# A fifth buffer of probabilities, the exponential ahead of the copies in even slots, early sign bits read a slot behind their product, row sums in six columns

## The chip, the core and the metric

One core of a Trainium2 chip runs the whole program. The engines named here are PE (TensorE's matmuls), PEld (its weight loads), DVE (VectorE), ACT (ScalarE), POOL (GpSimd) and SP (the queue that issues most of the DMAs). The metric is the device time of one execution in microseconds; a kernel's time is the median of several executions.

## What is computed

Attention within hash buckets, for 4 batches and 8 heads of 768 positions with 64 channels, and then a gated block on the 512 channels of the heads side by side:

```python
q_bits = (np.einsum('bhsd,dk->bhsk', q, proj) > 0)          # 6 signs; k_bits likewise
mask = q_bucket[:, :, :, None] == k_bucket[:, :, None, :]
scores = np.where(mask, scale * np.matmul(q, k.transpose(0, 1, 3, 2)), -1e9)
scores = scores - np.max(scores, axis=-1, keepdims=True)
attn = np.exp(scores)
attn = attn / (np.sum(attn, axis=-1, keepdims=True) + 1e-09)
x = np.matmul(attn, v)                                      # then heads side by side: B, 768, 512
gate = sigmoid(sum(conv_w[k] * shifted(x, k) for k in range(5)))
out = (gate * (x @ w_val)) @ w_out
```

## The kernel before

The work is cut into 192 tiles: 32 units (a batch and a head), and six tiles of 128 query rows in each. A tile's scores are 128 by 768. One loop runs over k, and what an iteration issues I call a slot. The order in which instructions are written is the order in which PE, ACT, DVE and POOL run them; SP's DMAs are ordered by a scheduler. Every engine takes its instructions strictly in turn, and one that waits holds all behind it.

A slot works on several tiles at once. In slot k:

- ACT copies the transposed probabilities of tile k-4 out of PSUM (`keep_transposed`, L348, two copies into `pt`).
- DVE takes the row maxima of tile k (`nm`, L297). In even slots it adds 1e-9 to the row sums of the pair k-2, k-1 (`row_sums`, L321, out of `sm` into `s1`; a profile names it `s`) and takes their reciprocals (`ri`, L325). It makes the factor `gs` (L303) and the shift `nb` (L307) of tile k.
- POOL scales the probabilities of tile k-2 by the reciprocals (L330).
- PE computes the scores of tile k+1 (L291) into one of two buffers `s`; the exponential of tile k-1 must have read that one.
- ACT takes the exponential of tile k (L315), with the shift as its bias, into a buffer `p`, and sums its rows on the way into `sm`. There are four `p` (`bufs=LAG + 1`, LAG is 3).
- PE takes a piece of other work: a piece of the gated block of an earlier batch (four matmuls, L424 or L449), in some early slots a product for sign bits, and in odd slots two steps of attention times values (L362, into `av`). DVE, POOL and ACT take pieces of weight conversion, convolution (L393) and so on.
- PE transposes the probabilities of tile k-3 (L339), three into each of two PSUM buffers `tp`; each must have been emptied by a copy of tile k-4.

When the last step of attention times values of a unit has been issued (an odd slot, k = 1 mod 6), ACT copies `av` into `x` (L370, two copies), behind that slot's exponential. So in the next even slot, k = 2 mod 6, these two copies stand ahead of whatever ACT does first.

The gated block of a batch can start when its eight heads are done, so up to about 190 us PE has no pieces of it. In those first slots the eight weight parts are converted on DVE, ACT and POOL, through the one PSUM buffer `m`.

The signs of q and k against the projections are folded into the scores as 12 more rows. For units 0 to 15 they come from `bits` (L229 the product into `m`, L232 the compare on DVE). For units 16 to 31 a generator, `early_bits`, makes them ahead of time: it loads four units' halves (L246), multiplies them (L251, into `m`), compares on DVE (L254, out of `m` into `ht`) and stores the result in DRAM (L256). It takes one step in each slot k with 6 <= k < 60 and k mod 6 in (3, 4); a step that multiplies also compares and stores.

An output block is copied out of PSUM into one of two buffers `o` (L455 on DVE, L457 on ACT) and stored by L459.

Of the kernel before, what the change touches and what calls it, by code (L numbers as in the profile page):

```python
# [8 lines left out]
FP32 = mybir.dt.float32  # L9
# [17 lines left out]
def kernel(  # L27
# [26 lines left out]
    vp = ctx.enter_context(tc.tile_pool(name="vp", bufs=2))  # L54
    pp = ctx.enter_context(tc.tile_pool(name="pp", bufs=LAG + 1))
    small = ctx.enter_context(tc.tile_pool(name="small", bufs=6))
# [5 lines left out]
    wst = ctx.enter_context(tc.tile_pool(name="wst", bufs=2))  # L62
    op = ctx.enter_context(tc.tile_pool(name="op", bufs=2))

# [171 lines left out]
    def early_bits():  # L236

        for i in range(16, len(units), 4):
            u = dram.tile([P, S], FP32, name="ud")
            rows = []  # L240
            for hf, name in enumerate(("hh", "hl")):
                yield
                rows.append([hp.tile([P, HS], FP32R, name=name).bitcast(FP32) for _ in range(4)])
                for jj, t in enumerate(rows[-1]):
                    b, h = units[i + jj]
                    nc.sync.dma_start(out=t, in_=qk[b, h, :, hf * HS:(hf + 1) * HS])  # L246
            for hf in range(2):
                yield
                z = ps_m.tile([P, 512], FP32, name="m")
                for jj, t in enumerate(rows[hf]):  # L250
                    nc.tensor.matmul(out=z[32 * jj:32 * jj + 32, 0:HS], lhsT=proj_sb, rhs=t, start=True, stop=True,  # L251
                                     tile_position=(0, 32 * jj))
                t = hp.tile([P, HS], FP32, name="ht", bufs=2)
                nc.vector.tensor_scalar(out=t.bitcast(FP32R), in0=z[:, 0:HS], scalar1=rows_sb[:, 0:1],  # L254
                                        scalar2=rows_sb[:, 1:2], op0=ALU.is_ge, op1=ALU.mult)
                nc.sync.dma_start(out=u[:, hf * HS:(hf + 1) * HS], in_=t)  # L256
            early[i] = u

# [50 lines left out]
    def exponentials(k):  # L309
        s, nb = ss.pop(k), nbs.pop(k)  # L310
        p = pp.tile([P, 2, HS], FP32, name="p")
        if k % 2 == 0:
            cur["sm"] = small.tile([P, 2, 2], FP32, name="sm")
        sm = cur["sm"]
        nc.scalar.activation(out=p, in_=s[:, :, 0:HS], func=AF.Exp, bias=nb, scale=gs.pop(k), accum_out=sm[:, k % 2, 0:1])  # L315
        ps[k] = (p.rearrange("p a b -> p (a b)"), sm)


    def row_sums(k):
        sums[k] = small.tile([P, 2, 2], FP32, name="s1")  # L320
        nc.vector.tensor_scalar(out=sums[k][:, :, 0], in0=ps[k][1][:, :, 0], scalar1=1e-9, scalar2=None, op0=ALU.add)  # L321

    def recip(k):
        ri = small.tile([P, 2], FP32, name="ri")
        nc.vector.reciprocal(out=ri, in_=sums.pop(k)[:, :, 0])  # L325
        rcs[k], rcs[k + 1] = ri[:, 0:1], ri[:, 1:2]
# [82 lines left out]
    def moe(b, xs_, g):  # L409
# [30 lines left out]
        def outp(o, tb):  # L440
# [4 lines left out]
            for hi, wi in ((0, 0), (0, 1), (1, 0)):  # L445
# [6 lines left out]
                later()  # L452
            ob = op.tile([P, 512], FP32, name="o")
            if cur["gates"]:
# [46 lines left out]
    with tc.manual_schedule(engines=ENGINES):  # L501
# [10 lines left out]
        step(weights[1])  # L512
        ahead = [early_bits()]
        for k in range(N + LAG + 1):
            if 0 <= k - LAG - 1:
                keep_transposed(k - LAG - 1)
# [18 lines left out]
            if k < N:  # L535
                exponentials(k)
            if k >= 60 or k % 2:
                step(convs)
# [9 lines left out]
            step(preps)  # L548
            if 6 <= k < 60 and k % 6 in (3, 4):
                step(ahead)  # L550
# [72 lines left out]
```

## Time and profile before

| | us |
|---|---|
| median of 3 runs (620.15 to 621.71) | 621.56 |
| the profiled execution | 621.24 |
| its span, from the first to the last instruction | 619.2 |
| PE busy in the span | 585.0 |
| PE idle until scores could overwrite a buffer that an exponential read | 16.9 |
| DVE busy | 434.5 |
| ACT busy | 420.3 |
| POOL busy | 387.6 |

The TensorE clock granted was 0.997 of full speed. In a row of the timeline stand the start in us from the span's start, the time taken, the engine, the line, the operation, the output and inputs, the count of instructions merged, and in brackets the engine's idle time ahead of it with what ended it. In a row of the waits stand who waited for whom, then the us in total, the number of times, and the longest.

### The profile page before, as it was taken

What the parts mean: (1) busy time and instruction counts of PE and PEld (TensorE: products, weight loads), DVE (VectorE), ACT (ScalarE), POOL (GpSimd) and SP (SyncE); (2) the same over time, 40 slices, a digit from 0 to 9 for tenths busy, and PEclk for the clock granted to TensorE, in tenths of its full rate; (3) what the DMA queues carried; (4) which work ended last, traced back from release to release, by engine and by line L of the source; (5) the groups of instructions that cost most, each with busy time, mean ns of one, the idle gap of its engine ahead of it and who ended that gap; (6) DMA issues with size and microseconds to landing.
All of it is one profiled execution on the core that took longest, in us unless ns stands there. A gap on an engine that the chain in (4) does not pass through costs nothing.

```text
span 619.2 us, 10665 instructions
## 1 busy us (share of the span) xinstructions
PE 585.0 (94%) x3496; PEld 421.4 (68%) x3496; DVE 434.5 (70%) x1017; ACT 420.3 (68%) x881; POOL 387.6 (63%) x373
## 2 busy tenths in 40 slices
PE   5799998989899999999999999999999999999997
PEld 2665655556567776776668787777667777775895
DVE  5787889898885866668575867668665877665532
ACT  2786777677778676777787676777787766765400
POOL 3575777677866765578665777468764776544321
PEclk9899999999999999999999999999999999999999
DMA  7575767473533334243434234333422213200111
GB/s 228 167 209 168 216 170 208 129 202 82 132 82 74 79 77 130 73 108 83 125 80 115 55 83 123 87 112 83 108 70 78 68 43 92 66 19 1 51 52 51
DMA packets 29030, 64.64 MB, mean 104 GB/s; under 512 B 4936, under 2 KB 10056, under 8 KB 28976
## 3 DMA queue, kind: packets, MB, share of 16 engines
q1 hardware_dynamic: 28832, 63.93, 37.7%
q8 instruction: 28, 0.46, 0.3%
q14 instruction: 26, 0.21, 0.1%
q10 hardware_dynamic: 144, 0.03, 0.0%
HBM read 30.60 MB, written 7.86 MB: 62 GB/s over the span
## 4 chain that ended last, share of the span: by engine, by line
PE 71%; ACT 14%; DVE 11%; issue 2%; DMA 2%; SPq 0%; POOL 0%; ACTq 0%; DVEq 0%; POOLq 0%
PE av L362 19%; PE s L291 17%; PE tp L339 13%; PE m L449 8%; PE m L424 7%; ACT p L315 6%; ACT pt L348 4%; DVE nm L297 3%; ACT x L370 2%; DVE g L393 2%; PE tp L424 1%; PE tp L449 1%; PE s L449 1%; PE m L229 1%; PE s L424 1%
## 5 line engine op out<-in xcount | busy, mean ns | idle before, releaser
L330 POOL TENSOR_SCALAR p<-p,ri 128x768 f32<-128x768 f32 x192 | 205.0, 1072 | 157.7 <-DVE nb L307 131.3
L297 DVE TENSOR_REDUCE nm<-s 128x1 f32<-128x768 f32 x192 | 182.6, 951 | 63.9 <-PE s L291 63.5
L348 ACT COPY pt<-tp 128x384 f32<-128x384 f32 x384 | 165.7, 485 | 81.7 <-PE tp L339 80.9
L315 ACT ACTIVATE p<-s,nb,gs 128x768 f32<-128x768 f32 x192 | 192.7, 1003 | 40.5 <-DVE nb L307 35.6
L339 PEld LDWEIGHTS tp<-ident,p 128*128 128x128 f32 x1152 | 129.2, 141 | 71.8 <-issue 45.2
L339 PE MATMUL tp<-ident,p 128*128 128x128 f32 x1152 | 163.8, 278 | 2.8 <-ACT pt L348 2.2
L362 PE MATMUL av<-pt,vt 128*64 128x384 f32 x768 | 144.9, 498 | 0.0
L291 PE MATMUL s<-ak,aq 76*128 76x384 f32 x384 | 117.7, 387 | 19.6 <-ACT p L315 16.9
L291 PE MATMUL s<-bk,bq 128*128 128x384 f32 x384 | 100.6, 343 | 0.4 <-DVE bq L277 0.4
L362 PEld LDWEIGHTS av<-pt,vt 128*64 128x64 f32 x768 | 46.9, 136 | 63.0 <-issue 62.9
L291 PEld LDWEIGHTS s<-ak,aq 76*128 76x128 f32 x384 | 59.0, 193 | 35.6 <-ACT p L315 31.8
L393 DVE SCALAR_TENSOR_TENSOR g<-x,cw_sb,g 128x768 f32<-128x768 f32 x64 | 77.3, 1208 | 2.2 <-POOL g L391 2.1
L291 PEld LDWEIGHTS s<-bk,bq 128*128 128x128 f32 x384 | 71.2, 192 | 0.8 <-issue 0.8
L198 POOL TENSOR_TENSOR bq<-r,aq 128x768 fp32r<-128x768 f32 x31 | 57.5, 1853 | 0.1
L435 POOL TENSOR_TENSOR hl<-ht,hh 128x384 fp32r<-128x384 f32 x32 | 32.2, 1006 | 39.4 <-DVE hh L433 39.4
L370 ACT COPY x<-av 64x384 f32<-64x384 f32 x64 | 30.4, 474 | 30.9 <-PE av L362 30.2
L383 POOL TENSOR_TENSOR xl<-x,xh 128x384 fp32r<-128x384 f32 x32 | 33.4, 1059 | 18.0 <-DVE xh L382 18.0
L424 PE MATMUL m<-xh,wv 128*128 128x384 f32 x200 | 42.7, 337 | 0.0
L307 DVE TENSOR_SCALAR nb<-nm,gs 128x1 f32<-128x1 f32 x192 | 40.2, 209 | 3.5
L315 ACT ACTIVATION_READ_ACCUMULATOR p<-s,nb,gs 128x1 f32 x192 | 39.1, 203 | 0.0
L429 DVE TENSOR_TENSOR ht<-m,g 128x384 f32<-128x384 f32 x25 | 13.9, 556 | 35.7 <-PE m L424 29.3
L449 PE MATMUL m<-wo,hh 128*128 128x512 f32 x144 | 38.1, 394 | 0.0
(86 smaller groups left out, 483.7 us busy)
## 6 DMA issues: line engine op xcount, KB each, us to landing
r<-in_qk_dram SPq DMA_DIRECT2D x32, 384.0 KB
vt<-in_v_dram SPq DMA_DIRECT2D x16, 384.0 KB
out_dram<-o SPq DMA_DIRECT2D x24, 256.0 KB
ak<-aq SPq DMA_DIRECT2D x31, 192.0 KB
bk<-aq SPq DMA_DIRECT2D x31, 192.0 KB
bk<-bq SPq DMA_DIRECT2D x31, 192.0 KB
bq<-aq SPq DMA_DIRECT2D x31, 192.0 KB
hh<-in_qk_dram SPq DMA_DIRECT2D x16, 192.0 KB
```

What stands on the lines that cost most here:

```text
L198: nc.gpsimd.tensor_tensor(out=bq, in0=r, in1=aq.bitcast(FP32), op=ALU.subtract)
L291: nc.tensor.matmul(out=s[:, hf, 0:HS], lhsT=lq[0:n, qs], rhs=rk[0:n, hf * HS:(hf + 1) * HS], start=n == M, stop=n == P)
L297: nc.vector.tensor_reduce(out=nm, in_=s[:, :, 0:HS], axis=AX.XY, op=ALU.max, negate=True)
L315: nc.scalar.activation(out=p, in_=s[:, :, 0:HS], func=AF.Exp, bias=nb, scale=gs.pop(k), accum_out=sm[:, k % 2, 0:1])
L330: nc.gpsimd.tensor_scalar(out=p, in0=p, scalar1=rcs.pop(k), scalar2=1.0, op0=ALU.mult, op1=ALU.mult)
L339: nc.tensor.transpose(out=tp[:, n * P:(n + 1) * P], in_=p[:, kb * P:(kb + 1) * P], identity=ident)
L348: nc.scalar.copy(out=pt[:, :, qo:qo + P], in_=tp[:, 0:HS].rearrange("p (a b) -> p a b", b=P))
L362: nc.tensor.matmul(out=av[s * D:(s + 1) * D, 0:HS], lhsT=vt[:, kb, hh * D:(hh + 1) * D], rhs=pt[kb // 3][:, kb % 3, :], start=(kb == 0), s ...
L370: nc.scalar.copy(out=x[hh * D:(hh + 1) * D, o:o + HS], in_=av[s * D:(s + 1) * D, 0:HS])
L393: nc.vector.scalar_tensor_tensor(out=g, in0=x[:, k:k + S], scalar=w, in1=g, op0=ALU.mult, op1=ALU.add)
L424: nc.tensor.matmul(out=acc[:, 0:HS], lhsT=wv[wi][:, c, j * P:(j + 1) * P], rhs=xs_[(c, o)][xi], start=(m == 0), stop=(m == 11))
L449: nc.tensor.matmul(out=acc, lhsT=hs[(o, j)][hi][:, tb * P:(tb + 1) * P], rhs=wo[wi][:, j, :], start=(m == 0), stop=(m == 11))
```

## The change

Five things change.

1. There are five buffers `p` instead of four, and one `o` instead of two. At the end of the program (`cur["end"]`) output blocks go through the `p` buffers.
2. In even slots `keep_transposed(k-4)` is issued behind the exponential of tile k. In odd slots it stays ahead.
3. `early_bits` has a step for the product and a step of its own for the compare and the store. The loads of a group are issued all eight at once, in the step of the last compare of the group before. The steps are taken in slots of a list `look`.
4. The row sums are written in six columns: the pair of sums three times over.
5. The reciprocal reads the first two of the six.

```diff
-    pp = ctx.enter_context(tc.tile_pool(name="pp", bufs=LAG + 1))
+    pp = ctx.enter_context(tc.tile_pool(name="pp", bufs=LAG + 2))
...
-    op = ctx.enter_context(tc.tile_pool(name="op", bufs=2))
+    op = ctx.enter_context(tc.tile_pool(name="op", bufs=1))
...
+        rows = rows_of(16)
+        for i in range(16, len(units), 4):
+            u = dram.tile([P, S], FP32, name="ud")
             for hf in range(2):
                 yield
+                z = product(rows[hf])
+                yield
                 t = hp.tile([P, HS], FP32, name="ht", bufs=2)
                 nc.vector.tensor_scalar(out=t.bitcast(FP32R), in0=z[:, 0:HS], scalar1=rows_sb[:, 0:1],
                                         scalar2=rows_sb[:, 1:2], op0=ALU.is_ge, op1=ALU.mult)
                 nc.sync.dma_start(out=u[:, hf * HS:(hf + 1) * HS], in_=t)
+            if i + 4 < len(units):
+                rows = rows_of(i + 4)
             early[i] = u
...
-        sums[k] = small.tile([P, 2, 2], FP32, name="s1")
-        nc.vector.tensor_scalar(out=sums[k][:, :, 0], in0=ps[k][1][:, :, 0], scalar1=1e-9, scalar2=None, op0=ALU.add)
+        sums[k] = small.tile([P, 6], FP32, name="s1")
+        nc.vector.tensor_scalar(out=sums[k], in0=ps[k][1][:, :, 0].unsqueeze(1).to_broadcast([P, 3, 2]), scalar1=1e-9,
+                                scalar2=None, op0=ALU.add)
...
-            ob = op.tile([P, 512], FP32, name="o")
+            if cur["end"]:
+                ob = pp.tile([P, 2, HS], FP32, name="p").rearrange("p a b -> p (a b)")[:, 0:512]
+            else:
+                ob = op.tile([P, 512], FP32, name="o")
...
+        look = [10] + [k for k in range(12, 50) if k % 6 in (3, 4) and k // 6 not in (3, 7)] + list(range(51, 59))
         for k in range(N + LAG + 1):
-            if 0 <= k - LAG - 1:
+            if 0 <= k - LAG - 1 and (k % 2 or k >= N):
                 keep_transposed(k - LAG - 1)
...
             if k < N:
                 exponentials(k)
+                if k % 2 == 0 and 0 <= k - LAG - 1:
+                    keep_transposed(k - LAG - 1)
...
-            if 6 <= k < 60 and k % 6 in (3, 4):
+            if k in look:
                 step(ahead)
```

Here `rows_of(i)` issues the eight loads of a group and `product(rows)` the four matmuls of a half into `m`.

ACT's order around the end of a unit's attention (slots k = 1, 2, 3 mod 6), before:

```order
L315 ACTIVATE p_835,sm_798<-s_792,nb_828,gs_825 128x768
L370 COPY x_605<-av_687 64x384 x2
L348 COPY pt_819<-tp_843 128x3x128
L348 COPY pt_820<-tp_847 128x3x128
L315 ACTIVATE p_869,sm_870<-s_830,nb_862,gs_857 128x768
L348 COPY pt_819<-tp_877 128x3x128
L348 COPY pt_820<-tp_881 128x3x128
L315 ACTIVATE p_899,sm_870<-s_864,nb_892,gs_889 128x768
```

And of the change:

```order
L325 ACTIVATE p_835,sm_796<-s_790,nb_828,gs_825 128x768
L381 COPY x_613<-av_692 64x384 x2
L325 ACTIVATE p_867,sm_868<-s_830,nb_860,gs_855 128x768
L359 COPY pt_819<-tp_843 128x3x128
L359 COPY pt_820<-tp_847 128x3x128
L359 COPY pt_819<-tp_877 128x3x128
L359 COPY pt_820<-tp_881 128x3x128
L325 ACTIVATE p_899,sm_868<-s_862,nb_892,gs_889 128x768
```

The exponential of the even slot now comes directly behind the two copies into `x`, and the four copies of two tiles' transposes follow each other.

PE's order at k = 15 and 16, with the first early product (`hh`), before:

```order
L229 MATMUL m<-r,proj_sb 32x384 x4
L362 MATMUL av<-pt,vt 64x384 x4
L339 MATMUL tp<-ident,p 128x128 x6
L291 MATMUL s<-ak,aq 128x384 x2
L291 MATMUL s<-bk,bq 128x384 x2
L251 MATMUL m<-hh,proj_sb 32x384 x4
L339 MATMUL tp<-ident,p 128x128 x6
```

And of the change:

```order
L229 MATMUL m<-r,proj_sb 32x384 x4
L250 MATMUL m<-hh,proj_sb 32x384 x4
L373 MATMUL av<-pt,vt 64x384 x4
L350 MATMUL tp<-ident,p 128x128 x6
L301 MATMUL s<-ak,aq 128x384 x2
L301 MATMUL s<-bk,bq 128x384 x2
L350 MATMUL tp<-ident,p 128x128 x6
```

The early product has moved from the even slot 16 into the odd slot 15, directly behind the other sign product into `m`.

DVE's order at k = 21 and 22, where a compare stood, before:

```order
L382 CAST xh<-x 128x384 x2
L254 TENSOR_SCALAR ht<-m,packed 128x384
L297 TENSOR_REDUCE nm<-s 128x1
L321 TENSOR_SCALAR s_937<-sm 128x2
L303 TENSOR_SCALAR gs<-nm 128x1
```

And of the change:

```order
L393 CAST xh<-x 128x384 x2
L307 TENSOR_REDUCE nm<-s 128x1
L331 TENSOR_SCALAR s_924<-sm 128x6
L313 TENSOR_SCALAR gs<-nm 128x1
L336 RECIPROCAL ri<-s_924 128x2
```

The compare has left this place, so nothing stands between the casts and the maxima of tile 22, and the row sums have their six columns.

More of the change, by code (lines that the diff above doesn't have):

```diff
@@ L236, in early_bits, with rows_of @@
     def early_bits():
-        for i in range(16, len(units), 4):
-            u = dram.tile([P, S], FP32, name="ud")
+        def rows_of(i):
             rows = []
             for hf, name in enumerate(("hh", "hl")):
-                yield
                 rows.append([hp.tile([P, HS], FP32R, name=name).bitcast(FP32) for _ in range(4)])
@@ L246, in early_bits, with product @@
                     nc.sync.dma_start(out=t, in_=qk[b, h, :, hf * HS:(hf + 1) * HS])
+            return rows
+        def product(rows):
+            z = ps_m.tile([P, 512], FP32, name="m")
+            for jj, t in enumerate(rows):
+                nc.tensor.matmul(out=z[32 * jj:32 * jj + 32, 0:HS], lhsT=proj_sb, rhs=t, start=True, stop=True,
+                                 tile_position=(0, 32 * jj))
+            return z
+        rows = rows_of(16)
+        for i in range(16, len(units), 4):
+            u = dram.tile([P, S], FP32, name="ud")
             for hf in range(2):
                 yield
[L249 to L252, printed above, removed]
+                z = product(rows[hf])
+                yield
                 t = hp.tile([P, HS], FP32, name="ht", bufs=2)
@@ L319, in row_sums @@
     def row_sums(k):
-        sums[k] = small.tile([P, 2, 2], FP32, name="s1")
-        nc.vector.tensor_scalar(out=sums[k][:, :, 0], in0=ps[k][1][:, :, 0], scalar1=1e-9, scalar2=None, op0=ALU.add)
+        sums[k] = small.tile([P, 6], FP32, name="s1")
+        nc.vector.tensor_scalar(out=sums[k], in0=ps[k][1][:, :, 0].unsqueeze(1).to_broadcast([P, 3, 2]), scalar1=1e-9,
+                                scalar2=None, op0=ALU.add)
     def recip(k):
         ri = small.tile([P, 2], FP32, name="ri")
-        nc.vector.reciprocal(out=ri, in_=sums.pop(k)[:, :, 0])
+        nc.vector.reciprocal(out=ri, in_=sums.pop(k)[:, 0:2])
         rcs[k], rcs[k + 1] = ri[:, 0:1], ri[:, 1:2]
```

## Prediction

> **What bounds the kernel now.** I read the busy time by stage first, then the waits, then single slots in the timeline. A slot is one tile k of the 192; "even" and "odd" are k's. The stages (columns: stretch in us, its length, then busy time of PE, PEld, DVE, ACT and POOL, clock, DMA share, GB/s):
>
> ```profile
> 20.00:190.00 170.00, 155.01 (x978) 99.90 (x978) 143.41 (x336) 129.54 (x278) 119.60 (x116) 0.99 0.56 156
> 190.00:560.00 370.00, 364.90 (x2203) 272.70 (x2200) 254.05 (x613) 272.01 (x572) 243.87 (x230) 1.00 0.33 84
> ```
>
> So TensorE sets the pace. Up to 190 us, before the second part's matmuls join, it idles 15.0 of 170 us and VectorE is close behind (84% busy). From 190 to 560 us it idles 5.1 of 370, and there only its own queue counts: whatever makes it wait once is not made up. The waits:
>
> ```profile
> ACT p L315 <- DVE nb L307: 35.6, 45, 6.0
> PE s L291 <- ACT p L315: 16.9, 34, 2.0
> DVE ht L254 <- PE m L251: 6.2, 6, 1.6
> PE tp L339 <- ACT pt L348: 2.2, 7, 0.8
> ```
>
> What the change goes after is in the second row: scores that wait for an exponential. What it may disturb is in the last: transposes wait almost never for ScalarE's copies.
>
> An ordinary even slot of the first stage (k=24), by engine:
>
> ```profile
> 73.00 0.87 PE L339 MATMUL tp<-ident,p 128*128 128x128 f32 x6
> 73.63 0.59 PE L291 MATMUL s<-ak,aq 76*128 76x384 f32 x2
> 74.41 0.82 PE L339 MATMUL tp<-ident,p 128*128 128x128 f32 x6
> 75.48 0.62 PE L291 MATMUL s<-ak,aq 76*128 76x384 f32 x2 [0.25 <-ACT p L315]
> ...
> 73.58 0.86 ACT L348 COPY pt<-tp 128x384 f32<-128x384 f32 x2 [0.68 <-PE tp L339]
> 74.33 1.01 ACT L315 ACTIVATE p<-s,nb,gs 128x768 f32<-128x768 f32 x1
> 75.31 0.87 ACT L348 COPY pt<-tp 128x384 f32<-128x384 f32 x2
> ...
> 72.54 0.81 DVE L321 TENSOR_SCALAR s<-sm 128x2 f32<-128x2 f32 x1
> 73.53 0.20 DVE L307 TENSOR_SCALAR nb<-nm,gs 128x1 f32<-128x1 f32 x1
> ```
>
> I call t the start of the transposes of tile k-4 (73.00). Then come scores k+1 (t+0.63), transposes k-3 (t+1.41) and scores k+2 (t+2.48). Unheld, these last would follow their transposes as the first pair do, after 0.63, so at t+2.04: 0.44 is lost to copies, then exponential (0.75 from one start to the next), then 1.15 from the exponential's start to the scores.
>
> **The change, part by part.** *Exponential first.* The order of the two does not free ScalarE: transposes k-3 need the copies of k-4 out of their two buffers, and scores k+2 stand behind those transposes on TensorE. The wait moves from the scores to the transposes. Its price comes from the rows above and these, where transposes did wait for a copy, and an exponential for its shift:
>
> ```profile
> 63.16 0.86 ACT L348 COPY pt<-tp 128x384 f32<-128x384 f32 x2
> 63.78 0.85 PE L339 MATMUL tp<-ident,p 128*128 128x128 f32 x6 [0.15 <-ACT pt L348]
> 70.97 0.21 DVE L307 TENSOR_SCALAR nb<-nm,gs 128x1 f32<-128x1 f32 x1
> 71.28 0.99 ACT L315 ACTIVATE p<-s,nb,gs 128x768 f32<-128x768 f32 x1
> ```
>
> Shift's end to exponential 0.10; exponential to copies 0.98 (74.33 to 75.31); copies to transposes 0.62; transposes to scores 0.63. So scores k+2 come 2.33 after the shift's end, where they came at t+2.48, or 1.25 after a late shift. At k=24 the shift ends at t+0.73. Without the 0.65 that its row sum took too long it would be t+0.08, and the scores would come at t+2.41: a gain of 0.07. Slots as good as that I put at ten: -0.7 us. That is the most the new order gives unless some other matmul fills the slot.
>
> *The slots behind a head's end* (k = 2 mod 6). Here ScalarE takes two copies out of the attention accumulator before it can start (k=80):
>
> ```profile
> 234.53 0.88 PE L339 MATMUL tp<-ident,p 128*128 128x128 f32 x6
> 236.89 0.82 PE L339 MATMUL tp<-ident,p 128*128 128x128 f32 x6
> 237.54 0.62 PE L291 MATMUL s<-ak,aq 76*128 76x384 f32 x2
> ...
> 234.65 0.97 ACT L370 COPY x<-av 64x384 f32<-64x384 f32 x2 [1.40 <-PE av L362]
> 235.64 0.86 ACT L348 COPY pt<-tp 128x384 f32<-128x384 f32 x2
> 236.39 1.01 ACT L315 ACTIVATE p<-s,nb,gs 128x768 f32<-128x768 f32 x1
> ```
>
> Now: scores at t+3.01. After: exponential from t+1.0, copies t+1.98, transposes t+2.60 instead of t+2.36, scores 0.57 to 0.63 behind (0.57 is the shortest follow-on that I see): t+3.17 to t+3.23, a loss of 0.16 to 0.22 that no DVE timing changes. There are 30 such slots, one for each head but the last two. Eight I leave out (two where sign products fill the slot, six late for another reason, below): 22 x 0.18 = +4.0 us.
>
> *Slots whose shift is late.* The worst kind (k=122), one of six such from 216 to 497 us:
>
> ```profile
> 355.84 0.88 PE L339 MATMUL tp<-ident,p 128*128 128x128 f32 x6
> 357.96 0.82 PE L339 MATMUL tp<-ident,p 128*128 128x128 f32 x6
> 358.85 0.62 PE L291 MATMUL s<-ak,aq 76*128 76x384 f32 x2
> ...
> 357.40 0.21 DVE L307 TENSOR_SCALAR nb<-nm,gs 128x1 f32<-128x1 f32 x1
> ```
>
> VectorE is behind with other work, and the shift ends (357.61) at t+1.77. Before, the copies did not care; scores came at t+3.01. After: t+1.77 + 0.10 + 0.98 + 0.62 + 0.57 = t+4.04, 1.03 later. Of the 63 even slots from 190 us on I find 27 with a shift later than t+0.5; priced singly, the six worst give 5.0 us and the rest 4.0. But TensorE's delay in one slot lets VectorE catch up for the next, so these do not add: bounds 2 and 9, and I take 4.0.
>
> *The row sums.* Of 96, most take 0.16 us, one 0.81:
>
> ```profile
> L321 DVE TENSOR_SCALAR s<-sm x96: 150/160/808, 17.6 to 561.9; 128x2 f32<-128x2 f32 x96
> L321 DVE TENSOR_SCALAR s<-sm 128x2 f32<-128x2 f32 x96 | 22.9, 238 | 6.8 <-ACT p L315 6.2
> 72.42 0.91 POOL L330 TENSOR_SCALAR p<-p,ri 128x768 f32<-128x768 f32 x1
> ```
>
> The long one began at 72.54 under a GpSimd instruction and ended (73.35) just behind it (73.33). Mean 238 less 160, times 96, is 7.5 us of VectorE time. The form with six columns is in no row here: it keeps all the waits, or none. I take none, as nothing else in the slot changes with its shape. The Trainium skill says why (SBUF — State Buffer, SBUF: two separate sides: a two-port VectorE operation and GpSimd hold one port pair exclusively; VectorE: DVE Perf Modes, What auto-detection actually checks: two ports are taken only if the outermost sizes of source and destination are both even, or equal). By it two columns to two take the pair and three rows to six do not; the rows above agree for the old form. By this rule the sum stands as below; if the six columns kept the waits it would be 2 higher.
>
> *The sign bits.* The compare (L254) no longer holds VectorE's queue for its product: 6.2 us of idle gone, behind which the next maxima and shift stood. All eight products now lie in odd slots, beside the attention product; the TensorE work is the same. But at k=15 and 39 the product now follows the other sign product (L229) directly, on the one buffer m, and must wait until VectorE has emptied it:
>
> ```profile
> 50.22 1.51 PE L362 MATMUL av<-pt,vt 128*64 128x384 f32 x8
> 50.36 0.68 DVE L232 TENSOR_SCALAR u<-m,packed 128x384 fp32r<-128x384 f32 x1 [0.29 <-PE m L229]
> ```
>
> What started at 50.22 now starts behind 51.04: +0.8, twice, +1.6 us (none if something else were the later wait there).
>
> *What the relief is worth.* 7.5 + 6.2 = 13.7 us of VectorE time, mostly before 190 us. It shortens only slots that VectorE holds, such as k=34:
>
> ```profile
> 100.05 0.87 PE L339 MATMUL tp<-ident,p 128*128 128x128 f32 x6
> 101.25 0.49 DVE L321 TENSOR_SCALAR s<-sm 128x2 f32<-128x2 f32 x1
> 101.85 0.19 DVE L307 TENSOR_SCALAR nb<-nm,gs 128x1 f32<-128x1 f32 x1
> ```
>
> The shift ends at t+1.99. Less 0.33 of its row sum and 1.0 of a compare's wait ahead of it (6.2 over 6), it would be t+0.66, and the scores come at t+2.99 instead of t+3.24 (1.25 behind the shift): 0.25 earlier. With a whole 0.65 it is 0.6. I find six slots of this stage so relieved, at 0.4: -2.4. Three late ones get nothing and pay 1.08 each, of which VectorE wins back half: +1.7. So -0.7 for the rest of this stage. Bounds: -8 if most of the 15.0 us that TensorE idles there goes, +4 if no relief arrives.
>
> *Nothing:* the fifth p buffer (it lets the exponential go ahead; that is priced above) and the one output buffer. The closest two output copies of the long stage, and the last store:
>
> ```profile
> 464.16 0.69 DVE L455 COPY o<-m 128x512 f32<-128x512 f32 x1 [3.75 <-PE m L449]
> 469.86 0.69 DVE L455 COPY o<-m 128x512 f32<-128x512 f32 x1 [3.71 <-PE m L449]
> 616.04 0.33 SPq L459 DMA_DIRECT2D out_dram<-o  x1
> ```
>
> That store took 3.1 us from issue to the end of the span (619.2), so the one behind 464.16 has landed by 468.0. Without this cover VectorE, or ScalarE with its exponentials behind it, would stand for the rest of those 3.1. The sign loads, now eight at once on SP's queue, slip in where it waited for GpSimd anyway: within 1 us either way, taken as nothing.
>
> Sum: -0.7 + 4.0 + 4.0 + 1.6 - 0.7 = **+8.2 us** on the profiled execution's 621.24 (span 619.2 and 2.0 around it), so 629.4. That execution lies 0.3 under the median of 621.56, within the spread of the three runs; I say **629**.
>
> **The rivals.**
> 1. *VectorE was the bound up to 190 us* (84% busy; 45 exponentials wait for a shift). The relief then brings 8 of the 13.7 us, and early shifts bring the head-end and late slots down to +3: 616. Against it: the best slot gains 0.07. 0.24.
> 2. *Both wash out*, the late slots cost 2, the head ends 2 and the relief brings 5: 619.5 to 623. 0.15.
> 3. *Late shifts feed on themselves*: in each late slot the exponential now holds the copies, the transposes, the scores and so the next maxima. Decided where a shift ends later than t+0.2 without VectorE catching up: 9 instead of 4, and +4 up to 190 us: 638. 0.11.
> 4. *The six columns still wait for GpSimd* (the change doesn't do what it says): half the relief goes, +2, inside the forecast's range.
>
> **Chances.** The forecast, 624 to 634 by itself: 0.50. Faster by over 0.3% (1.9 us, about what a measurement of this kernel can tell from no change) 0.24, within it 0.15, slower 0.61. Range 616 to 636: it takes in half of rival 1 and all of rival 2, and leaves out half of 1 and most of 3.
>
> **What would show it.** Right: scores waiting for exponentials (16.9) nearly gone, and in their place transposes waiting for ScalarE's copies, 2.2 now, at 10 us or more; TensorE's idle time from 190 us on up from 5.1 to 9 or more over as many slots; row sums all near 0.16; the compare waiting for nothing; idle time on TensorE before the early product at k=15. Wrong: transposes that still never wait, which would mean shifts end by t+0.2 everywhere; or TensorE idle for under 9 us up to 190 us, rival 1.

## The result, and the profile after

| | before | changed |
|---|---|---|
| median, us | 621.54 | 637.94 (637.0 to 639.16) |
| ratio, 95% interval | | 1.0271 (1.025 to 1.0292) |
| span of the profiled execution, us | 619.2 | 637.0 |
| PE busy in the span, us | 585.0 | 586.0 |

The changed kernel is slower by 16.4 us. The direction is the one forecast, but the time lies above the range (616 to 636), and the loss is more than twice the one predicted (7.5). TensorE has the same work as before; nearly all of the difference is time in which it stands idle: 51.0 us of the span instead of 34.2, so 16.8 of the 17.8 us by which the two spans differ. The granted clock is at most a small part of it: it was 0.997 in the profiled execution before and 0.986 in that of the changed kernel, but another execution of the changed kernel, at 0.997, took 637.42 us all the same. The stages of the changed kernel (columns as in the prediction):

```profile
20.00:190.00 170.00, 148.84 (x936) 96.05 (x937) 136.92 (x327) 125.30 (x268) 116.56 (x113) 0.97 0.56 155
190.00:560.00 370.00, 354.82 (x2136) 263.14 (x2133) 244.93 (x595) 267.45 (x555) 234.93 (x223) 1.00 0.33 84
```

Up to 190 us TensorE idles 21.2 us where it idled 15.0; from 190 to 560 us 15.2 where it idled 5.1. The waits of the changed kernel:

```profile
ACT p L325 <- DVE nb L317: 67.5, 84, 6.1
PEld tp L350 <- POOL p L341: 33.8, 37, 1.9
PE tp L350 <- ACT pt L359: 28.4, 42, 1.8
...
PE s L301 <- ACT p L325: 2.6, 3, 1.4
...
DVE ht L262 <- PE m L250: 1.3, 1, 1.3
```

Scores that wait for an exponential went from 16.9 to 2.6 us, as the change intends. Transposes that wait for a copy went from 2.2 to 28.4. More is paid than is saved. Where it is paid shows when TensorE's idle stretches over 0.06 us are summed by the slot in which they fall (us; a slot starts with the transposes of tile k-4, and the column of k = 3 holds 4.3 us from the start of the program):

| slots, k mod 6 | 0 | 1 | 2 | 3 | 4 | 5 | sum |
|---|---|---|---|---|---|---|---|
| before | 0.4 | 5.8 | 5.7 | 10.3 | 0.1 | 3.3 | 25.6 |
| changed | 10.0 | 0.0 | 22.3 | 7.2 | 2.7 | 0.0 | 42.2 |

The odd slots, behind an exponential that came late, lost nearly all their waits (of the 7.2 in k = 3, 4.3 are the start and 2.5 the products for sign bits at k=15, 39 and 57). The even ones got new ones, and the slots behind a head's end (k = 2 mod 6) most. There the changed kernel at k=80, from its timeline in order of time, t = 242.87:

```profile
242.87 0.88 PE L350 MATMUL tp<-ident,p 128*128 128x128 f32 x6
242.98 0.97 ACT L381 COPY x<-av 64x384 f32<-64x384 f32 x2 [1.41 <-PE av L373]
...
243.98 0.99 ACT L325 ACTIVATE p<-s,nb,gs 128x768 f32<-128x768 f32 x1
...
244.96 0.85 ACT L359 COPY pt<-tp 128x384 f32<-128x384 f32 x2
...
245.57 0.85 PE L350 MATMUL tp<-ident,p 128*128 128x128 f32 x6 [0.19 <-ACT pt L359]
...
246.18 0.59 PE L301 MATMUL s<-ak,aq 76*128 76x384 f32 x2
```

Exponential at t+1.11, copies at t+2.09, transposes at t+2.70, scores at t+3.31; before, the scores came at t+3.01. Where no matmuls of the gated block stand between, the wait is in full view (k=26, t = 81.33):

```profile
81.33 0.88 PE L350 MATMUL tp<-ident,p 128*128 128x128 f32 x6
...
82.44 0.99 ACT L325 ACTIVATE p<-s,nb,gs 128x768 f32<-128x768 f32 x1
...
84.03 0.85 PE L350 MATMUL tp<-ident,p 128*128 128x128 f32 x6 [1.11 <-ACT pt L359]
```

### The profile page after: what moved, and what is told of

It is laid out like the page before. It is cut to its first block, busy times and chain, and to the rows that moved or that the text cites. A ratio compares the mean times of both kernels' runs of the same rounds, so it can differ in the third digit from the quotient of the medians.

```text
span 637.0 us, 10613 instructions
## 1 busy us (share of the span) xinstructions
PE 586.0 (92%) x3496; PEld 421.6 (66%) x3496; DVE 429.9 (67%) x1017; ACT 424.3 (67%) x881; POOL 385.0 (60%) x373
## 4 chain that ended last, share of the span: by engine, by line
PE 65%; DVE 17%; ACT 10%; POOL 3%; issue 3%; DMA 1%; ACTq 0%; POOLq 0%; SPq 0%; DVEq 0%
PE av L373 16%; PE tp L350 15%; PE s L301 14%; PE m L460 7%; ACT p L325 6%; DVE nm L307 6%; PE m L435 6%; DVE g L404 4%; POOL p L341 2%; ACT pt L359 2%; ACT x L381 2%; DVE nb L317 1%; PE tp L435 1%; PE tp L460 1%; PE s L460 1%
## 5 line engine op out<-in xcount | busy, mean ns | idle before, releaser
L341 POOL TENSOR_SCALAR p<-p,ri 128x768 f32<-128x768 f32 x192 | 201.8, 1055 | 170.5 <-DVE nb L317 160.6
L350 PE MATMUL tp<-ident,p 128*128 128x128 f32 x1152 | 166.7, 282 | 33.7 <-ACT pt L359 28.4
L301 PE MATMUL s<-bk,bq 128*128 128x384 f32 x384 | 102.2, 348 | 0.4 <-DVE bq L287 0.4
L301 PEld LDWEIGHTS s<-bk,bq 128*128 128x128 f32 x384 | 72.5, 196 | 0.8 <-issue 0.8
L440 DVE TENSOR_TENSOR ht<-m,g 128x384 f32<-128x384 f32 x25 | 13.9, 556 | 41.7 <-PE m L435 34.5
L325 ACT ACTIVATION_READ_ACCUMULATOR p<-s,nb,gs 128x1 f32 x192 | 37.6, 196 | 0.0
```

Of the source, the lines that this page charges most:

```text
L301: nc.tensor.matmul(out=s[:, hf, 0:HS], lhsT=lq[0:n, qs], rhs=rk[0:n, hf * HS:(hf + 1) * HS], start=n == M, stop=n == P)
L341: nc.gpsimd.tensor_scalar(out=p, in0=p, scalar1=rcs.pop(k), scalar2=1.0, op0=ALU.mult, op1=ALU.mult)
L350: nc.tensor.transpose(out=tp[:, n * P:(n + 1) * P], in_=p[:, kb * P:(kb + 1) * P], identity=ident)
```

## The experiments

The change has three separable parts: the order (with the buffers that it needs), the sign bits, and the row sums. Four runs took them apart.

### Copies ahead in every slot, the rest kept

```diff
-            if 0 <= k - LAG - 1 and (k % 2 or k >= N):
+            if 0 <= k - LAG - 1:
                 keep_transposed(k - LAG - 1)
...
-                if k % 2 == 0 and 0 <= k - LAG - 1:
-                    keep_transposed(k - LAG - 1)
```

> The changed kernel with the copies ahead of the exponential in every slot again; its five buffers, its sign bits and its row sums stay. Theory A (the order alone makes the kernel slower: in the changed kernel TensorE idles 22.3 us in the slots k = 2 mod 6 and 10.0 us in k = 0 mod 6, where it idled 5.7 and 0.4): the loss goes, and what is left is the relief of VectorE, less some 2 us that the early products at k = 15 and 39 wait: 615 to 621 us. Theory B (the sign bits and row sums, whose work now meets other work, carry a good part of the 16 us): 626 us or more. Theory C (the order had a gain of its own in the odd slots that is lost with it): 621 to 626 us.

Measured: 622.11 us, 1.0018 of before (1.0002 to 1.0034). Its stages:

```profile
20.00:190.00 170.00, 155.83 (x970) 101.06 (x969) 138.93 (x335) 126.90 (x277) 119.09 (x116) 0.98 0.55 155
190.00:560.00 370.00, 364.82 (x2202) 272.30 (x2201) 251.43 (x611) 271.86 (x571) 241.24 (x230) 1.00 0.33 85
```

The long stage is back at 5.2 us of idle time. So the order costs 15.8 us in the changed kernel, and the other parts together win nothing: 622.11 is 1.1 above the kernel before as measured beside it (621.01). By its number that is theory C's interval, just above A's. C's reason, a gain of the order that is lost with it, is not needed for it: in the two runs below the row sums alone and the sign bits alone add up to -0.4 us, which within the intervals is what is left here. What A had wrong was the relief.

### The order alone

The kernel before with the fifth `p`, the one `o` and the new order; sign bits and row sums as before.

```diff
-    pp = ctx.enter_context(tc.tile_pool(name="pp", bufs=LAG + 1))
+    pp = ctx.enter_context(tc.tile_pool(name="pp", bufs=LAG + 2))
...
-            if 0 <= k - LAG - 1:
+            if 0 <= k - LAG - 1 and (k % 2 or k >= N):
                 keep_transposed(k - LAG - 1)
...
                 exponentials(k)
+                if k % 2 == 0 and 0 <= k - LAG - 1:
+                    keep_transposed(k - LAG - 1)
```

> The kernel before with the fifth buffer of probabilities, the one output buffer and the exponential ahead of the copies in even slots, and nothing else of the change. Theory A: the whole loss is here, and without VectorE's relief more shifts are late, so 638 to 643 us, transposes wait for copies by 28 us or more. Theory B: under 632 us, since the other two parts carry the rest.

Measured: 641.46 us, 1.0335 (1.0311 to 1.036). Its waits:

```profile
ACT p L315 <- DVE nb L307: 65.8, 78, 6.0
...
PE tp L339 <- ACT pt L348: 35.5, 47, 2.0
```

Theory A. Without VectorE's relief the order costs 20.4 us instead of 15.8. So the parts do not simply add: under the new order the row sums and sign bits win some 4 us (1.0271 against 1.0335), and with the copies ahead nothing.

### Row sums in six columns alone

```diff
-        sums[k] = small.tile([P, 2, 2], FP32, name="s1")
-        nc.vector.tensor_scalar(out=sums[k][:, :, 0], in0=ps[k][1][:, :, 0], scalar1=1e-9, scalar2=None, op0=ALU.add)
+        sums[k] = small.tile([P, 6], FP32, name="s1")
+        nc.vector.tensor_scalar(out=sums[k], in0=ps[k][1][:, :, 0].unsqueeze(1).to_broadcast([P, 3, 2]), scalar1=1e-9,
+                                scalar2=None, op0=ALU.add)
```

> The kernel before with the row sums in six columns alone. The row sums' 7.5 us of waiting for GpSimd go. If VectorE sets the pace of the slots up to 190 us (first rival of the prediction): 614 to 617 us. If TensorE does and only late slots gain: 619 to 621 us. If nothing there was on the path: 621.5 us.

Measured: 618.21 us, 0.9955 (0.9939 to 0.9971): 2.8 us faster, between the middle case (619 to 621) and VectorE as the bound (614 to 617), and nearer the middle. The group of these instructions in this run (columns: busy us, mean ns, idle ahead of them):

```profile
L321 DVE TENSOR_SCALAR s<-sm 128x6 f32<-128x6 f32 x96 | 14.5, 151 | 6.9 <-ACT p L315 6.6
```

Their time fell from 22.9 to 14.5 us. Of 8.4 us of VectorE time some 2.8 reached the end.

### The sign bits alone

```diff
+                yield
+                z = product(rows[hf])
+                yield
                 t = hp.tile([P, HS], FP32, name="ht", bufs=2)
...
-            if 6 <= k < 60 and k % 6 in (3, 4):
+            if k in look:
```

> The kernel before with the sign bits' new steps alone. The prediction's own terms: two products that wait for the buffer m, +1.6 us, against the compare's 6.2 us of waiting: 620 to 623 us. If the compare's wait was on the path: 617 us or less. If the eight loads at once hold back other loads: 624 us or more.

Measured: 623.46 us, 1.0048 (1.0033 to 1.0064). By 0.5 above the interval that my own terms gave, and slower than before. The trace shows two costs. One is the product directly behind the other one into `m` (in the changed kernel, k=15):

```profile
53.91 0.68 DVE L232 TENSOR_SCALAR u<-m,packed 128x384 fp32r<-128x384 f32 x1 [0.29 <-PE m L229]
...
54.65 0.85 PE L250 MATMUL m<-hh,proj_sb 128*32 128x384 f32 x8 [0.80 <-DVE u L232]
```

The other I had priced at nothing: the loads. In the sign bits' own run, whose profiled execution (626.88 us) was the longest of ten, the last two loads of a half are issued from 164.49 on, the product could have gone on at 167.36, and it waits:

```profile
164.49 1.10 SPq L244 DMA_DIRECT2D hl<-in_qk_dram  x2
...
166.52 0.84 PE L250 MATMUL m<-hl,proj_sb 128*32 128x384 f32 x4
169.02 1.99 PE L250 MATMUL m<-hl,proj_sb 128*32 128x384 f32 x4 [1.66 <-DMA hl<-in_qk_dram]
```

The list of slots ends with the steps at 51 to 58 in a row. The loads of a group are issued in the step of the last compare of the group before, for the last group in slot 54: one slot ahead of its first product (k=55) and three ahead of the one that waits here (k=57). The earlier groups have at least five slots. The size of this wait differs from kernel to kernel: the product at k=57 waits 1.66 us here, 1.14 in the changed kernel with the copies ahead, and 0.31 in the changed kernel itself.

### Sign bits later, but with their products in the old places

Row sums in six columns, copies ahead everywhere, and

```diff
-        look = [10] + [k for k in range(12, 50) if k % 6 in (3, 4) and k // 6 not in (3, 7)] + list(range(51, 59))
+        look = [10] + [k + d for k in range(16, 58) if k % 12 in (4, 9) for d in (0, 1)]
```

> The kernel before with the row sums in six columns and the sign bits' compare and store one slot behind their product, but the products in the slots in which they stood before (16, 21, 28, 33, 40, 45, 52, 57), so that none stands behind the other sign product and each group's loads have five slots. Beside 618.2 us with the six columns alone. Theory A (the places of the products and loads made the sign bits dear, the later compare is worth a little): 616.5 to 618.5 us. Theory B (the later compare itself, or eight loads at once, costs): 619.5 us or more.

Measured: 616.26 us, 0.992 (0.9902 to 0.9939). Theory A. Next to 0.9955 with the six columns alone, reading the product a slot later is worth some 2 us where the places are right (the two intervals just touch). It cost 2.45 where they were not. This is the fastest kernel of the study, and faster than both.

### The buffers without the order

The kernel just above (the fastest) with five `p` and one `o`.

```diff
-    pp = ctx.enter_context(tc.tile_pool(name="pp", bufs=LAG + 1))
+    pp = ctx.enter_context(tc.tile_pool(name="pp", bufs=LAG + 2))
...
-    op = ctx.enter_context(tc.tile_pool(name="op", bufs=2))
+    op = ctx.enter_context(tc.tile_pool(name="op", bufs=1))
```

> The kernel with early products in their old places and six columns, with the fifth buffer of probabilities and the one output buffer, but the copies ahead in every slot. It tells whether the 3 us by which the kernel with the exponential first in ten slots was slower are the order's. Theory A (the order's): 615.5 to 617 us, as without the buffers. Theory B (the buffers'): 618 us or more.

Measured: 617.39 us, 0.9938 (0.9923 to 0.9954). It is 0.4 above what theory A allowed, but its interval overlaps that of the kernel without the buffers (0.9923 to 0.9954 and 0.9902 to 0.9939), and the lengths of their slots agree to 0.02 us in nearly all of them behind slot 10. I read it as no difference that can be told.

### The head's-end slots spared

The changed kernel with the copies ahead in k = 2 mod 6 as well:

```diff
-            if 0 <= k - LAG - 1 and (k % 2 or k >= N):
+            if 0 <= k - LAG - 1 and (k % 2 or k % 6 == 2 or k >= N):
...
-                if k % 2 == 0 and 0 <= k - LAG - 1:
+                if k % 2 == 0 and k % 6 != 2 and 0 <= k - LAG - 1:
```

> The changed kernel with the copies ahead again in the slots behind a head's end (k = 2 mod 6) alone; in the other even slots the exponential stays first. Theory A (the slots behind a head's end are the larger part, since ScalarE starts there 0.9 us later than elsewhere): their 22.3 us of TensorE idle time fall to the 4.5 us that they have with the copies always ahead, and 6.4 come back in the odd slots k = 3 mod 6: 637.9 - 17.8 + 6.4 = 626.5, so 625 to 629 us. Theory B (late shifts in the other even slots feed on themselves and carry most of it): 631 us or more. Theory C (the late shifts in the other even slots come only from the delay at the head ends): 622 us or less.

Measured: 628.86 us, 1.0129 (1.0111 to 1.0148). Theory A: the head's ends are the larger part, 9.1 of the 15.8 us. (This run has the copies ahead at k=8 too, where no head ends yet; the idle time there falls from 1.52 to 0.25 us.) The idle time in the slots k = 2 mod 6 is 3.9 us, and 14.7 stay in the other even slots. Its waits lie between the two kernels:

```profile
PE tp L350 <- ACT pt L359: 12.9, 24, 1.3
...
PE s L301 <- ACT p L325: 7.2, 15, 1.6
```

### The copies of x taken out of the way

The changed kernel, but behind a head's end ScalarE takes the exponential, then the copies of the transposes, then the two copies into `x`:

```diff
+        yield
         if hh == 0:
...
                 if k % 2 == 0 and 0 <= k - LAG - 1:
                     keep_transposed(k - LAG - 1)
+                    if k % 6 == 2:
+                        step(avs)
```

> The changed kernel with the two copies out of the attention accumulator moved behind the copies of the transposed probabilities in the slots k = 2 mod 6, so that the exponential there has nothing ahead of it on ScalarE. Theory A (the two copies ahead are what makes these slots dear): exponentials start up to 0.9 us earlier in some 30 slots where the shift is early enough, so 10 to 15 us of the idle time go: 624 to 629 us. Theory B (it only passes on: the two copies then hold the next slot's copies and exponential, or the next head's accumulator): 633 us or more.

Measured: 647.52 us, 1.0421 (1.0398 to 1.0445), slower still. Theory B by its time, but not by its reason. The slots k = 2 mod 6 did get better: 11.4 us of idle time instead of 22.3. What replaced it stands in k = 4 mod 6, 19.0 instead of 2.7:

```profile
ACT p L325 <- DVE nb L317: 102.0, 95, 6.0
...
DVE xh L394 <- ACT x L382: 35.6, 12, 7.6
```

VectorE's casts of `x` stand in its queue ahead of maxima and shift. They waited 11.0 us for ScalarE's copies in the changed kernel, and 35.6 here; the shifts behind them were late, and with them the exponentials. So the copies were delayed for the first head of each pair only, whose half of `x` nobody reads before the second head is done:

```diff
+        if hh == 0:
+            yield
         if hh == 0:
...
+            if k % 12 == 2:
+                step(avs)
```

> The changed kernel with the two copies out of the accumulator behind exponential and transposed copies (as in the run that came to 647.5 us), but only for the first head of a pair, whose half of x nobody reads before the second head is done. Theory A (two copies ahead of the exponential make these slots dear, and that run lost again because VectorE's casts of x, and with them the shifts behind, had to wait for copies that came a slot's half later): the idle time in the slots k = 2 mod 12 falls by about 4 us, in those with an early shift, and VectorE's casts wait no longer than in the changed kernel (11.0 us): 633 to 636 us. Theory B (late copies out of the accumulator hold ScalarE's next slot whoever reads them): 638 us or more.

Measured: 636.55 us, 1.026 (1.0243 to 1.0277), against 1.0271 (1.025 to 1.0292) of the changed kernel: half a microsecond above what theory A allowed, and not a difference that these intervals settle. The trace is clearer:

```profile
PE tp L350 <- ACT pt L359: 24.6, 43, 1.8
...
DVE xh L394 <- ACT x L382: 11.1, 5, 6.4
```

Casts wait as little as in the changed kernel. The idle time in k = 2 mod 12 falls by 3.1 us up to the last exponential, where about 4 was expected, and it falls where the shift is early: from k on, the even slot and the odd one behind it are shorter by 0.91 and 0.92 us at k=26 and 50, 0.62 at 86, 0.59 at 158, 0.39 at 134 and 182. Others whose shift is later (62, 74, 110) gain nothing. That the two copies ahead of the exponential make these slots dear is shown where the shift is early; that moving them pays is not.

### The same move without the new order

In the fastest kernel (616.26 us), copies ahead everywhere, the copies of `x` of a pair's first head behind the exponential.

```diff
                 exponentials(k)
+            if k % 12 == 2:
+                step(avs)
```

> The kernel with early products in their old places and six columns (616.3 us), copies ahead in every slot, and in it the two copies out of the accumulator behind the exponential for the first head of a pair alone. There scores still wait 0.42 us in most odd slots behind a head's end of the first stage, 2.3 us in the six slots k = 3 mod 12 in which they do. Theory A: those waits go and nothing else starts to wait: 613.5 to 615.5 us. Theory B (ScalarE is then late for the copies of the odd slot or for the accumulator): 616 us or more.

Measured: 616.15 us, 0.9922 (0.9905 to 0.9938): no difference to 616.26, so theory A fails. There is no trace of this kernel that can be laid beside the others, so why the waits did not turn into time stays open.

### The new order only where the shift is early

The fastest kernel with five `p` and one `o` (617.39 us), and with the exponential first in k = 4 mod 6 below 60 alone. These are ten slots. In the changed kernel eight of the nine shifts from k=10 on end before t+0.1; that of k=4 ends at t+1.64 in both kernels.

```diff
-            if 0 <= k - LAG - 1:
+            if 0 <= k - LAG - 1 and not (k < 60 and k % 6 == 4):
...
+                if k < 60 and k % 6 == 4 and 0 <= k - LAG - 1:
+                    keep_transposed(k - LAG - 1)
```

> As the kernel with the products in their old places and six columns, with five buffers of probabilities and one output buffer, and with the exponential ahead of the copies only in the slots k = 4 mod 6 below 60, in most of which the changed kernel's shift ends before t+0.1 and its transposes waited for nothing. Theory A (where the shift is that early the order is a small gain, because scores in the odd slot behind no longer wait, some 1.5 us): 1 to 2 us under the kernel without it. Theory B (the order never gains): the same or up to 2 us over it.

Measured: 619.33 us, 0.9978 (0.9964 to 0.9992), 2 us over the kernel with the buffers and 3 over the one without. In this kernel most of the shifts are no longer early: at k=34 the shift ends at t+1.12 (t = 100.16), where in the changed kernel it ended at t-0.07.

```profile
100.16 0.88 PE L350 MATMUL tp<-ident,p 128*128 128x128 f32 x6
...
101.07 0.21 DVE L317 TENSOR_SCALAR nb<-nm,gs 128x1 f32<-128x1 f32 x1
...
101.40 0.99 ACT L325 ACTIVATE p<-s,nb,gs 128x768 f32<-128x768 f32 x1 [1.71 <-PE s L301]
...
102.99 0.84 PE L350 MATMUL tp<-ident,p 128*128 128x128 f32 x6 [1.25 <-POOL p L341]
```

(The bracket of the transposes names GpSimd; by the times the copies, from 102.38, were the last to come: the probabilities that are transposed here had been scaled by 96.97.)

One could put the changed kernel's early shifts down to time that TensorE loses in the two even slots ahead, in which VectorE catches up. The run with the copies ahead, where the order costs nothing there, shows that this holds for a part of them only. The ends of the shifts, from t:

| k | 10 | 16 | 22 | 28 | 34 | 40 | 46 | 52 | 58 |
|---|---|---|---|---|---|---|---|---|---|
| changed kernel | -1.06 | -0.97 | 0.07 | -0.72 | -0.07 | -0.98 | 0.73 | -0.72 | -2.63 |
| changed, copies ahead | 1.42 | -0.97 | 0.07 | -0.47 | 0.62 | -0.98 | 1.52 | -0.47 | -2.76 |
| buffers without the order | 1.40 | 0.69 | -0.71 | 0.30 | 1.12 | 1.23 | 1.69 | 0.60 | -0.35 |

Only at 10 and 34 is the shift early with the lost time and late without it (at 46 it is less late). At 16, 28, 40, 52 and 58 it is about as early without; what differs between the last two rows is where the early products and their compares stand.

Slot by slot against the kernel with the buffers only, the pair of slots from k on: at 22 and 58, with shifts at t-0.71 and t-0.35, it is 0.51 shorter; at 4, 10, 34 and 46, with t+1.64, t+1.40, t+1.12 and t+1.05, it is 0.97, 0.99, 0.79 and 0.42 longer (0.4 of the 0.97 at k=4 is a lower clock at the start, 0.50 until 26.8 us here and until 25.1 there). (16, 28, 40 and 52 hold an early product here, which hides part of the wait: 0.07, 0.00, 0.60 and 0.00 with t+0.69, t+0.34, t+1.22 and t+0.30.) Neither theory holds as it stands: the order gains where the shift is early and loses where it is late, and of the early ones most were not early any more.

### The new order from slot 60 on

An account made beforehand, slot by slot, from the changed kernel against the one with the copies ahead, tried on a kernel that has nothing of the first stage's trouble: the fastest kernel with five `p` and one `o`, exponential first in even slots from 60 on.

```diff
-            if 0 <= k - LAG - 1:
+            if 0 <= k - LAG - 1 and (k % 2 or k < 60 or k >= N):
...
+                if k % 2 == 0 and k >= 60:
+                    keep_transposed(k - LAG - 1)
```

> The kernel with early products in their old places, six columns and five buffers (617.4 us), with the exponential first in even slots from slot 60 on alone. The account made from the changed kernel's trace beside that with the copies ahead: 0.28 for each of the 22 slots behind a head's end, two of them with 2 more in all by a late shift, and 2.8 in the other even slots, 11.4 us together; it has nothing of the stage before. Theory A (the price belongs to the slots, whatever came before): 617 + 11.4, so 627 to 630 us, and TensorE's busy time from 190 to 560 us near 355. Theory B (lateness from the first 60 slots feeds the later ones): under 625 us.

Measured: 628.44 us, 1.012 (1.0096 to 1.0145). Theory A. Its stages:

```profile
20.00:190.00 170.00, 158.10 (x995) 103.36 (x995) 142.75 (x343) 132.30 (x282) 120.50 (x117) 0.98 0.56 158
190.00:560.00 370.00, 355.55 (x2140) 262.58 (x2138) 245.68 (x596) 265.98 (x557) 234.11 (x224) 1.00 0.32 84
```

Against the kernel with the buffers only, the pairs of slots below 60 differ by 0.1 us in sum, and slots 60 to 191 take 10.85 us longer. By place, from slot 60 on: 8.4 us in k = 2 mod 6 (account: 8.6), 1.9 in k = 0 (2.3), 0.5 in k = 4 (0.5). Both sides hold one slot, k=98, that costs 2.2 or 2.3 us, over half of it by a lower clock: in this run it was 0.50 of full speed from 288.60 to 292.00 us, in the changed kernel see below.

## Why the prediction was right in sign and half the size

Its direction and its mechanism held. The step that failed is the price of the new order: its terms (-0.7, +4.0, +4.0 and +1.7) made 9.0 us, and it cost 15.8. Furthest too low were the slots behind a head's end (4.0 put, 5.8 measured) and the even slots of the first stage (1.0 put, some 3.3 measured). The other parts, put at -2.4 for the relief and +1.6 for the products, so -0.8, came to +0.6.

The lengths of pairs of slots (from the start of an even slot to that of the next even one) in the changed kernel, less those in the one with the copies ahead, add up to 16.6 us, as the two profiled executions differ (639.16 and 622.50):

| slots, k mod 6 | 0 | 2 | 4 | sum |
|---|---|---|---|---|
| below 60 | +4.3 | +3.3 | -2.3 | +5.2 |
| from 60 on | +2.3 | +8.6 | +0.5 | +11.4 |

Two of these pairs hold something besides waits. In this execution of the changed kernel the granted clock was 0.50 of full speed from 35.20 to 38.60 us and from 298.00 to 301.40 us, right behind two waits of transposes (1.27 us at k=8, 1.81 at k=98); in the other execution it was 1.00 in these slots. For the same matmuls TensorE was busy 1.50 and 1.23 us longer in the two pairs, some 2.7 us of the 16.6. Whether such a wait brings the lower clock is not shown: the run with the copies of `x` behind for the first head alone has the same wait at k=98 (1.83 us), kept its clock, and its pair there is 1.33 us shorter.

1. **The wait moves from the scores to the transposes.** Right: 16.9 to 2.6 us in the one, 2.2 to 28.4 in the other. The links of its chain measured at k=80 as given: 0.98, 0.61 and 0.61.
2. **The slots behind a head's end: 22 x 0.18 = +4.0.** The place was right, the price too low. From slot 60 on it is 0.28 (18 of 22 slots lie between 0.26 and 0.30), and 0.28 to 0.30 in five of the first stage too. The error is in "exponential from t+1.0": the copies of `x` quoted there run from 234.65 to 235.62, which is t+1.09, and the exponential then starts at t+1.11, as in nearly every such slot. The same chain from there gives 0.27 to 0.33. The 22 slots so priced came to 16 x 0.28 from slot 60 on and 1.3 in the first stage, 5.8 us. That the two slots with sign products (14 and 38) pay nothing was right: 0.02 and 0.00.
3. **Late shifts from 190 us on: +4.0, bounds 2 and 9.** Inside its bounds, and a little low: 11.4 us from slot 60 on less the 16 x 0.28 above are 6.9. Of these 0.9 lie in slots 60 to 64, ahead of the 63 that I had counted, and 1.2 are the lower clock at k=98, which leaves 4.8. More slots pay than I took (70, 88, 108, 120, 168), and the six late head ends pay their 0.28 as well. The remark that TensorE's delay lets VectorE catch up holds at the very slot that was priced (k=122, t = 369.42):

```profile
369.42 0.87 PE L350 MATMUL tp<-ident,p 128*128 128x128 f32 x6
...
370.39 0.21 DVE L317 TENSOR_SCALAR nb<-nm,gs 128x1 f32<-128x1 f32 x1
...
370.70 1.00 ACT L325 ACTIVATE p<-s,nb,gs 128x768 f32<-128x768 f32 x1 [0.20 <-DVE nb L317]
...
372.30 0.84 PE L350 MATMUL tp<-ident,p 128*128 128x128 f32 x6 [0.60 <-ACT pt L359]
```

   The shift ends at t+1.18, not t+1.77, and the slot pays 0.45 instead of 1.03. Three others of that kind (74, 110, 146) pay no more than 0.29. The dearest is k=98, at 2.16: there the shift ends at t+1.70 and the transposes come at t+3.39, as the chain says, and 1.23 us of it are the clock.
4. **Ten good even slots: -0.7, "the most the new order gives".** Too low. I held a shift at t+0.08 for the best possible. With shifts from t-0.35 on down a slot gains 0.5, as at 22 and 58 in the run with ten slots. In the changed kernel k = 4 mod 6 gained 3.3 us from k=10 to 58. 2.5 of it are at 16, 28, 40, 52 and 58, where the shifts are early without the order too; the 1.0 at 10 and 34 came with time lost in the slots ahead.
5. **The rest of the first stage: -0.7.** The relief is real, more than the 2.4 that I took and less than its 13.7 us suggest: 2.8 us from the row sums, some 2 from the later compare where the products keep their places, both without the new order. The late slots cost more than the 1.7 that I had for three of them: 4.3 in k = 0 mod 6, 0.9 at k=4, and 2.0 at k=8, of which 1.5 are the clock's; k = 4 mod 6 gives 3.3 back from k=10 on. (At k=4 and 6 up to 1.0 more may be the clock's: at the start it was 0.50 until 28.4 us in the changed kernel and until 25.2 in the other.)
6. **The sign bits: +1.6 for products that wait for `m`.** The wait is there, 0.80 at k=15 as priced and 1.35 at k=39, so 2.15 in all. The loads, "within 1 us either way, taken as nothing", held in the changed kernel, where a product waited 0.31 us for one; it waited 1.14 with the copies ahead and 1.66 in the part's own run. That part alone cost 2.45 us.
7. **Row sums near 0.16.** Right; in the changed kernel (columns: least, median and longest in ns, first and last start):

```profile
L331 DVE TENSOR_SCALAR s<-sm x96: 142/150/164, 17.2 to 579.7; 128x6 f32<-128x6 f32 x96
```

   None of the 96 is stretched, where 17 took over 300 ns before. Rival 4 is out. This agrees with the rule of the Trainium skill that the prediction named (VectorE: DVE Perf Modes, What auto-detection actually checks).
8. **The buffers: nothing.** No run tells them from nothing.

In sum: of the 16.6 us that the order cost in the profiled executions, 2.7 are the lower clock in two pairs, which no term held. The other 13.9 stand against 9.0: the head ends are short by 1.8 (5.8), the late shifts from 190 us on by 0.8 (4.8), the first stage's gains and late slots by 2.3 (3.3 instead of -0.7 + 1.7). All three were low, because each late or delayed slot was priced at its barest and the slots not named at nothing. The other parts came to +0.6 (622.11 against 621.54; +1.1 against the 621.01 measured beside it) where +1.6 - 2.4 = -0.8 had been put. Together that is the miss: 16.4 against 8.2.

Rival 3 named the time (638), and its cause is not borne out from slot 60 on: nothing of the first 60 slots feeds the later ones (10.85 us in the run without them, 11.4 in the account), and the late shift at k=122 came earlier, not later. In the first stage it is not excluded: at k=30, 42 and 54 the shift ends at t+1.45, t+1.19 and t+0.69 in the changed kernel and at t+0.44, t+0.70 and t-0.35 with the copies ahead, and these three pay 1.26, 1.00 and 0.49 us. What makes them later stays open. Rival 1, VectorE as the bound up to 190 us, is out: it had the relief at 8 us and the head-end and late slots at 3, and the runs show 4 to 5 us of relief (in the fastest kernel) and 15.8 us of cost. Rival 2 had about that relief, but late slots and head ends at 2 each.

## What to carry to other kernels

Here a new order of two operations on a strictly ordered engine moved a wait rather than removed it. Ask what both consumers wait for: here the operation put back (copies) fed the engine that sets the pace as much as the one put ahead, and the order pays only where the input of the one put ahead is early. Earliness seen in a trace is a state of that kernel: here it came from where other work stood and, in some slots, from time lost just ahead, and it was gone in a kernel without them.

Price a repeated slot from the end of the row in front, not from a rounded time: 0.1 us too little in a slot that comes 28 times is 3 us. When steps are moved, count the slots that their loads get, not only the loads. And look at the granted clock of a slot before its length is put down to a wait.

## What I had not expected of the hardware

The six-column add takes no longer than the two-column one where neither waits (150 ns median in the changed kernel, 160 in the row of before), so three times the elements cost nothing here, and the long ones (up to 808 ns) are gone. And in the run with the sign bits alone, loads issued from 164.49 on were too late for a product that could have used them at 167.36: it waited until 169.02.

In the changed kernel the granted clock fell to 0.50 for 3.4 us in the middle of the program, twice, each time right behind a wait of TensorE of 1.3 or 1.8 us. The same wait stands in another run without such a fall, so the wait alone does not settle it.
